# Issuing the K and V loads of a decode-attention kernel from GpSimd in place of SyncE

## The chip, the core and the metric

The kernel runs on one core of a Trainium2 chip. A core has five engines with instruction streams of their own, which meet only at semaphores: TensorE (PE: matmuls; PEld is its weight load), VectorE (DVE), ScalarE (ACT), GpSimd (POOL) and SyncE (SP), which issues transfers and computes nothing. The transfers between the device memory (DRAM) and the on-chip memory (SBUF, 128 partitions) are run by 16 DMA engines. Whoever issues a transfer puts it on a queue of its own: SP, ACT and POOL each have one. A transfer adds 16 to a semaphore when it has landed.

The metric is the device time of one execution in microseconds (us), the median of several runs.

## What is computed

One token is decoded by a gated mix of two parts: attention over a cache of 65536 keys and values for each of 32 heads, and a small feed-forward part.

```python
# x [1,1,512]; k_cache, v_cache [1,32,65536,128] bf16; wq [512,4096]; wo [4096,512]
q = (x @ wq).reshape(B, Sq, H, Dh).transpose(0, 2, 1, 3)
scores = jnp.einsum("bhqd,bhkd->bhqk", q, k_cache) * (Dh ** -0.5)
p = softmax(scores, axis=-1)
a = jnp.einsum("bhqk,bhkd->bhqd", p, v_cache).transpose(0, 2, 1, 3).reshape(B, Sq, H * Dh) @ wo
b = (silu(x @ w_gate) * (x @ w_up)) @ w_down          # 512 -> 1792 -> 512
g = sigmoid((x * gate_w).sum(-1, keepdims=True))
return g * a + (1 - g) * b
```

K and V together are 32 x 2 x 65536 x 128 x 2 bytes = 1074 MB, read once. Nearly everything that moves is K and V.

## The kernel before

**Tiles.** The keys of a head are cut into two halves of 32768 (A and B). A half of K or V is one load of 8 MB: each of the 128 partitions gets 256 rows of 128 numbers, 64 KB in one piece. The loads go to four regions of one SBUF buffer called `ring`: K_A, K_B, V_A, V_B. The regions overlap (K_B begins in the middle of K_A, V_B 16 KB into V_A), so a load has to wait until the part of its neighbour that it overwrites has been used.

**Work of one head.** DVE transposes K chunk by chunk, 16 chunks of 16 rows for each half (line 309, into four buffers `kt`), and counts them in the semaphore `ktd`, 32 to a head. PE turns each chunk into scores (line 396, into `psS`). After both halves DVE takes the maximum along each partition (line 333), POOL takes it across the partitions (line 213), ACT makes the exponentials with their sums (lines 246 and 248), POOL adds the sums across partitions (line 215), and DVE transposes the exponentials into `pb` (line 335). Then PE multiplies them with V: half A at once (line 412 in `flow`; the semaphore `va1` says that the rows from 64 on have been used), half B after the scores of the first K half of the next head (lines 412, 447 and 403; the semaphore `vbd` says that V_B has been used).

**PE's order.** PE goes through blocks: `pe_ka` (scores of half A), `pe_vb` (values of half B of the head before), `pe_kb` (scores of half B, then values of half A). Between the `pe_vb` of head 30 and the `pe_kb` of head 31 it goes through `pe_wo`: it waits for both halves of the matrix wo, does 32 matmuls with the outputs of heads 0 to 30 (line 423 in `whole`), and raises `s_wod`. After the `pe_kb` of head 31 comes `pe_mlp`, the feed-forward part, and then a last `pe_vb`.

```python
            with nc.body("pe_wo", valid_engines=only):
                pe.wait_ge(sm["s_otn"], H + 1)
                ...
                pe.wait_ge(sm["s_wo"], 32)
                for j in range(32):
                    last = whole(om[:, j:j + 1], wo_ap[:, j, :], first=(j == 0))
                last.then_inc(sm["s_wod"], 1)
                nc.br("pe_kb", engines=only)
```

**SP's order.** SP issues every large load, one after the other, each behind a wait: wq first, then K of head 0 in four half loads, V_A of head 0, and then for each head r (`head` in the listing) the K_A of head r + 1 (when half of K_B has been transposed), the V_B of head r (after `va1`), the K_B of head r + 1 (when half of K_A has been transposed), the V_A of head r + 1 (after `vbd`). For the last round the two halves of wo stand ahead of the K_B of head 31, each behind a wait for transposes that free its place. Then follow, as their places come free, the weights w_gate and w_up (after `s_wod`), the last rows of wo, w_down, and the V_B of head 31 in six pieces (`PARTS`): the first, 64 rows per partition, at once, and the other five after `va1` of head 31. Since all of them are on one queue, they move in this order.

**POOL's order.** It clears some buffers, copies four tiles into `sel` (line 208), and then does the two reductions of each head, each behind its wait. The other changes of place, and the lines that issue and wait, are in the listing.

Of the kernel before, what the change touches and what calls it, by code (L numbers as in the profile page):

```python
# [6 lines left out]
KB = 1024  # L7
CH = 16
NB = 4
K_A, K_B = 0, 32 * KB  # L10
V_A, V_B = 96 * KB, 112 * KB
# [6 lines left out]
ET = mybir.EngineType  # L18
# [8 lines left out]
def bass_gated_mix__mha_block_cached__swiglu_ffn__decode_kernel(  # L27
# [11 lines left out]
    out: bass.AP,  # L39
):  # L40
    _, H, S, Dh = A_k_cache.shape
    D = A_wq.shape[0]
    F = B_w_gate.shape[1]
    Dc = D // P
    FC = F // P
    ROWS = S // (2 * P)
    NCH = ROWS // CH
    SCALE = float(Dh) ** -0.5
    assert Dh == 128 and D == 512 and F % P == 0 and ROWS == 256 and H == 32
    L = H - 1  # L50
    A_ORDER = list(range(NCH // 2, NCH)) + list(range(NCH // 2))
    B_ORDER = list(range(NCH))
    PER = 2 * NCH

    with ExitStack() as ctx:
# [6 lines left out]
        def sem(name):  # L62
            return ctx.enter_context(nc.semaphore(name))
# [46 lines left out]
        sm = {n: sem(n) for n in names.split()}  # L110
# [4 lines left out]
        kv_dram = {"k": A_k_cache[0].rearrange("h (u p r) d -> h u p (r d)", u=2, p=P),  # L115
                   "v": A_v_cache[0].rearrange("h (u p r) d -> h u p (r d)", u=2, p=P)}

        def at(byte, n):
            return ring[:, byte // 2:byte // 2 + n]

        WQ, WO, WG, WU, WO1, WD = 144 * KB, 0, 0, 14 * KB, 28 * KB, 64 * KB
        PARTS = ((192, 256), (0, 64), (64, 128), (128, 168), (168, 184), (184, 192))
        FLOW = 3
        MARKS = ("s_vb", "s_p2", "s_p3", "s_p4", "s_p5", "s_p6")
# [16 lines left out]
        @block.sync  # L141
        def _(sp):
            def load(dst, src, s):
                sp.dma_start(dst, src).then_inc(sm[s], 16)  # L144

            def place(kind, h, u, s):
                byte = {"k": (K_A, K_B), "v": (V_A, V_B)}[kind][u]
                src = kv_dram[kind][:, u]
                if isinstance(h, int):
                    src = src[h]  # L150
                else:
                    src = src[bass.ds(h, 1)].rearrange("h p n -> (h p) n")
                load(at(byte, ROWS * Dh), src, s)

            k0 = kv_dram["k"][0, 0]
            k1 = kv_dram["k"][0, 1]
            half = ROWS * Dh // 2
            load(at(K_A + 2 * half, half), k0[:, half:2 * half], "s_ka")
            load(at(K_A, half), k0[:, 0:half], "s_k0a")
            load(at(K_B + 2 * half, half), k1[:, half:2 * half], "s_k0b")  # L160
            sp.wait_ge(sm["ktd"], NCH // 2)
            load(at(K_B, half), k1[:, 0:half], "s_kb")
            sp.wait_ge(sm["s_q"], 1)
            place("v", 0, 0, "s_va")

            def head(r, late):
                sp.wait_ge(sm["ktd"], r * PER + (PER - NCH // 2))
                place("k", r + 1, 0, "s_ka")
                sp.wait_ge(sm["va1"], r + 1)
                place("v", r, 1, "s_vb")  # L170
                if late:
                    wo_dram = A_wo.rearrange("(p j) n -> p (j n)", j=32)
                    for q in range(2):
                        sp.wait_ge(sm["ktd"], r * PER + (PER + 3 * NCH // 4 + q * NCH // 4))
                        load(at(WO + q * 16 * KB, 16 * D), wo_dram[:, q * 16 * D:(q + 1) * 16 * D], "s_wo")
                sp.wait_ge(sm["ktd"], r * PER + (PER + NCH // 2))
                place("k", r + 1, 1, "s_kb")
                sp.wait_ge(sm["vbd"], r + 2)
                place("v", r + 1, 0, "s_va")

            with nc.Fori(0, L - 1, engines=[ET.SP]) as i:
                head(i, False)
            head(L - 1, True)
            sp.wait_ge(sm["s_wod"], 1)
            load(at(WG, Dc * F), B_w_gate.rearrange("(p c) f -> p (c f)", c=Dc), "s_wg")
            load(at(WU, Dc * F), B_w_up.rearrange("(p c) f -> p (c f)", c=Dc), "s_wu")
            load(at(WO1, D), A_wo[L * Dh:H * Dh, :], "s_wo1")
            sp.wait_ge(sm["ktd"], PER * H)
            wd_dram = B_w_down.rearrange("(p c) n -> p (c n)", c=FC)
            load(at(WD, WD_CUT * D), wd_dram[:, 0:WD_CUT * D], "s_wd")  # L190
            last = kv_dram["v"][L, 1]
            for n, ((r0, r1), s) in enumerate(zip(PARTS, MARKS)):
                if n == 1:
                    sp.wait_ge(sm["va1"], H)
                load(at(V_B + r0 * 256, (r1 - r0) * Dh), last[:, r0 * Dh:r1 * Dh], s)
            for j, s in ((FC - 3, "s_wd1"), (FC - 2, "s_wd2"), (FC - 1, "s_wd3")):
                load(at(WD + 2 * j * D, D), wd_dram[:, j * D:(j + 1) * D], s)

        @block.gpsimd
        def _(pool):  # L200
            nc.gpsimd.memset(xTz[:], 0.0).then_inc(sm["s_qd"], 1)
            nc.gpsimd.memset(qd[:], 0.0).then_inc(sm["s_qd"], 1)
            for m, n in enumerate(MARKS[1:]):
                nc.gpsimd.memset(hbuf[:, m], 0.0).then_inc(sm[n], 16 * L)
            pool.wait_ge(sm["s_id"], 1)
            for je in range(4):
                off = 64 * (je // 2) + je % 2
                last = nc.gpsimd.tensor_copy(sel[:, je, :].rearrange("p (g d) -> p g d", g=4),
                                             ident[:, off:off + 63:2].unsqueeze(1).to_broadcast([P, 4, 32]))
            last.then_inc(sm["s_sel"], 1)  # L210
            for h in range(H):
                pool.wait_ge(sm["s_mx"], h + 1)
                nc.gpsimd.partition_all_reduce(amx, mxs, P, RMAX).then_inc(sm["s_ar"], 1)  # L213
                pool.wait_ge(sm["s_exp"], h + 2)
                nc.gpsimd.partition_all_reduce(Lt, rsum, P, RADD).then_inc(sm["s_L"], 1)  # L215

        @block.scalar
        def _(act):
# [330 lines left out]
```

## Time and profile before

| | us |
|---|---|
| median of 3 runs | 2518.72 (2518.53 to 2519.13) |
| the profiled execution, first to last instruction (its own time) | 2517.1 |
| DVE busy | 1249.7 (50%) |
| PE busy | 1500.6 (60%) |
| POOL busy | 25.5 (1%) |
| moved by the DMA queues | 1087.86 MB, mean 432 GB/s |

All times within the profile are microseconds from the start of this one execution. Rows of the timeline give the start, the duration, the engine, the line of the kernel, the operation with what it writes and reads, how many instructions were merged, and in brackets how long the engine had been idle before and what ended that. "SPq" and "ACTq" are issues of transfers: their duration is that of the issue, not that of the transfer, and a merged row spans the waits between its issues. A "q" with a number is a DMA queue: q1 is SP's, q10 ACT's.

### The profile page before, as it was taken

What the parts mean: (1) busy time and instruction counts of PE and PEld (TensorE: products, weight loads), DVE (VectorE), ACT (ScalarE), POOL (GpSimd) and SP (SyncE); (2) the same over time, 40 slices, a digit from 0 to 9 for tenths busy, and PEclk for the clock granted to TensorE, in tenths of its full rate; (3) what the DMA queues carried; (4) which work ended last, traced back from release to release, by engine and by line L of the source; (5) the groups of instructions that cost most, each with busy time, mean ns of one, the idle gap of its engine ahead of it and who ended that gap; (6) DMA issues with size and microseconds to landing.
All of it is one profiled execution on the core that took longest, in us unless ns stands there. A gap on an engine that the chain in (4) does not pass through costs nothing.

```text
span 2517.1 us, 25084 instructions
## 1 busy us (share of the span) xinstructions
PE 1500.6 (60%) x10126; PEld 572.7 (23%) x10126; DVE 1249.7 (50%) x1213; ACT 42.4 (2%) x141; POOL 25.5 (1%) x79
## 2 busy tenths in 40 slices
PE   4664654755656556556565575565655655656566
PEld 1221221212222222222222221222221222222222
DVE  5454553644545536445455354464553544545534
ACT  0000000000000000000000000000000000000000
POOL 0000000000000000000000000000000000000000
PEclk9877877877778777777787787777877778778778
DMA  9999999999999999999999999999999999999999
GB/s 419 435 434 436 433 434 433 434 434 434 433 433 433 434 433 433 433 433 433 432 433 433 433 433 433 433 433 433 433 433 433 433 433 433 434 433 433 433 432 395
DMA packets 20892, 1087.86 MB, mean 432 GB/s; under 512 B 2323, under 2 KB 2838, under 8 KB 3094
## 3 DMA queue, kind: packets, MB, share of 16 engines
q1 hardware_dynamic: 20880, 1087.78, 99.9%
q8 instruction: 4, 0.07, 0.0%
q14 instruction: 2, 0.02, 0.0%
q10 hardware_dynamic: 6, 0.00, 0.0%
HBM read 1087.77 MB, written 0.00 MB: 432 GB/s over the span
## 4 chain that ended last, share of the span: by engine, by line
DMA 75%; DVE 15%; issue 7%; PE 2%; DVEq 1%; SPq 0%; ACT 0%; POOL 0%
DMA ring<-in_A_k_cache_dram 74%; DVE kt L309 15%; PE psS L396 2%; DMA ring<-in_A_v_cache_dram 1%; DVEq L306 0%; SPq L144 0%; PE psW L412 0%; DVE st L320 0%; PE psY L418 0%; PE psO L403 0%; ACT pa L248 0%; DVE pb L335 0%; DVE st L333 0%; DVEq L319 0%; DVE fin L354 0%
## 5 line engine op out<-in xcount | busy, mean ns | idle before, releaser
L396 PE MATMUL psS<-kt,zq 128*128 128x512 bf16 x4096 | 1134.0, 426 | 865.1 <-DVE kt L309 847.0
L309 DVE STREAM_TRANSPOSE kt<-ring 128x1024 uint32<-128x1024 uint32 x1024 | 1163.2, 1206 | 939.9 <-DMA ring<-in_A_k_cache_dram 939.9
L396 PEld LDWEIGHTS psS<-kt,zq 128*128 128x128 bf16 x4096 | 387.2, 104 | 1598.5 <-DVE kt L309 1134.7
L412 PE MATMUL psW<-ring,pb 128*4 128x512 bf16 x3584 | 255.2, 447 | 104.0 <-DVE pb L335 102.3
L412 PEld LDWEIGHTS psW<-ring,pb 128*4 128x4 bf16 x3584 | 94.2, 98 | 263.4 <-issue 186.7
L322 DVE COPY brow<-psW 128x512 f32<-128x512 f32 x32 | 22.1, 690 | 120.4 <-PE psW L412 120.4
L403 PEld LDWEIGHTS psO<-pb,ring 128*128 128x128 bf16 x2048 | 57.0, 98 | 0.6 <-DMA ring<-in_A_v_cache_dram 0.5
L403 PE MATMUL psO<-pb,ring 128*128 128x1 bf16 x2048 | 56.6, 163 | 0.4 <-DMA ring<-in_A_v_cache_dram 0.2
L325 DVE TENSOR_SCALAR lt<-psO,st,sc 128x4 f32 x32 | 9.4, 294 | 89.2 <-PE psO L403 89.2
L447 PE MATMUL psO<-id,brow 128*128 128x1 f32 x256 | 33.7, 253 | 25.5 <-DVE brow L322 24.7
L335 DVE STREAM_TRANSPOSE pb<-pa 128x512 bf16<-128x512 bf16 x32 | 22.8, 711 | 48.7 <-ACT pa L248 48.7
L246 ACT ACTIVATE st<-st 128x1 f32<-128x1 f32 x32 | 6.5, 203 | 2383.2 <-POOL st L213 2383.2
L333 DVE TENSOR_REDUCE st<-psS 128x1 f32<-128x512 f32 x32 | 22.1, 692 | 37.5 <-PE psS L396 37.5
L447 PEld LDWEIGHTS psO<-id,brow 128*128 128x128 f32 x256 | 31.0, 191 | 41.7 <-DVE brow L322 40.4
L213 POOL PARTITION_ALL_REDUCE st<-st x32 | 11.2, 350 | 2420.6 <-DVE st L333 2420.6
L248 ACT ACTIVATE pa<-psS,st 128x512 bf16<-128x512 f32 x32 | 22.0, 687 | 1.0
L215 POOL PARTITION_ALL_REDUCE st<-st x32 | 12.3, 383 | 36.4 <-ACT pa L248 36.4
L423 PE MATMUL psF<-ring,om 128*1 128x512 bf16 x32 | 9.6, 474 | 2.8 <-DMA ring<-in_A_wo_dram 2.8
L253 ACT COPY zq<-qd 128x16 bf16 x31 | 7.7, 248 | 0.0
L248 ACT ACTIVATION_READ_ACCUMULATOR pa<-psS,st 128x1 f32 x32 | 6.2, 193 | 0.0
L423 PE MATMUL psF<-ring,kt 128*1 128x512 bf16 x11 | 3.9, 527 | 3.0 <-DVE kt L348 3.0
L350 DVE COPY brow<-psW 128x512 f32<-128x512 f32 x1 | 0.7, 690 | 9.8 <-PE psW L412 9.8
(82 smaller groups left out, 48.9 us busy)
## 6 DMA issues: line engine op xcount, KB each, us to landing
ring<-in_A_k_cache_dram SPq DMA_DIRECT2D x4, 4096.0 KB, 27.6
ring<-in_A_v_cache_dram SPq DMA_DIRECT2D x3, 2048.0 KB, 17.9
ring<-in_A_wq_dram SPq DMA_DIRECT2D x1, 4096.0 KB, 12.1
ring<-in_A_wo_dram SPq DMA_DIRECT2D x2, 2048.0 KB, 10.6
ring<-in_B_w_gate_dram SPq DMA_DIRECT2D x1, 1792.0 KB, 33.2
ring<-in_B_w_up_dram SPq DMA_DIRECT2D x1, 1792.0 KB, 37.2
ring<-in_B_w_down_dram SPq DMA_DIRECT2D x1, 1408.0 KB, 13.4
ring<-in_A_v_cache_dram SPq DMA_DIRECT2D x1, 1280.0 KB, 21.5
```

The source lines that it names most:

```text
L213: nc.gpsimd.partition_all_reduce(amx, mxs, P, RMAX).then_inc(sm["s_ar"], 1)
L215: nc.gpsimd.partition_all_reduce(Lt, rsum, P, RADD).then_inc(sm["s_L"], 1)
L248: nc.scalar.activation(pa[:], psS[:], ACT.Exp, bias=nbias, scale=SCALE, accum_out=rsum).then_inc(sm["s_exp"], 1)
L309: nc.vector.transpose(o, src).then_inc(sm["ktd"], 1)
L322: nc.vector.tensor_copy(brow[:], psW[:]).then_inc(sm["s_flc"], 1)
L333: nc.vector.reduce_max(mxs, psS[:], AX_X).then_inc(sm["s_mx"], 1)
L335: nc.vector.transpose(pb[:], pa[:]).then_inc(sm["s_pb"], 1)
L396: last = nc.tensor.matmul(psS[:], zw[je][c], ktb[n % NB][:, je // 2, :, je % 2], start=first and je == 0, stop=stop and je == 3)
L403: last = nc.tensor.matmul(psO[:, 0:1], at(base + r * 256, Dh), pb[:, col:col + 1], start=first and n == 0, stop=stop and n == len(rows) - 1)
L412: last = nc.tensor.matmul(psW[g:g + 4, :], pb[:, col:col + 97:32], at(base + r * 256, 4 * Dh), start=first and n < 4, stop=stop and n >= l ...
L423: return nc.tensor.matmul(psF[0:1, :], lhs, rhs, start=first, stop=stop)
L447: nc.tensor.matmul(psO[:, 0:1], brow[:, e * Dh:(e + 1) * Dh], id4[:, e:e + 1], start=e == 0, stop=False)
```

## The change

All K loads and all V loads but the last five pieces are issued by POOL, which also writes their descriptors (the lists of what is to be moved). POOL's program is written out for all heads: after the clearing and the copies into `sel` come the four half loads of K of head 0 and its V_A, and then for each round the four loads, with the same waits as on SP, and the two reductions of the head between the first of them and the second. The first piece of the last V follows on POOL without a wait, ahead of the reductions of head 31. SP keeps wq, both halves of wo (each behind its wait for transposes, but no longer in the row of the K loads), the weights of the feed-forward part, and the last five pieces of V after `va1` of head 31.

```diff
         @block.sync
...
-            def head(r, late):
-                sp.wait_ge(sm["ktd"], r * PER + (PER - NCH // 2))
-                place("k", r + 1, 0, "s_ka")
-                sp.wait_ge(sm["va1"], r + 1)
-                place("v", r, 1, "s_vb")
-                if late:
-                    wo_dram = A_wo.rearrange("(p j) n -> p (j n)", j=32)
-                    for q in range(2):
-                        sp.wait_ge(sm["ktd"], r * PER + (PER + 3 * NCH // 4 + q * NCH // 4))
-                        load(at(WO + q * 16 * KB, 16 * D), wo_dram[:, q * 16 * D:(q + 1) * 16 * D], "s_wo")
-                sp.wait_ge(sm["ktd"], r * PER + (PER + NCH // 2))
-                place("k", r + 1, 1, "s_kb")
-                sp.wait_ge(sm["vbd"], r + 2)
-                place("v", r + 1, 0, "s_va")
-
-            with nc.Fori(0, L - 1, engines=[ET.SP]) as i:
-                head(i, False)
-            head(L - 1, True)
+            wo_dram = A_wo.rearrange("(p j) n -> p (j n)", j=32)
+            for q in range(2):
+                sp.wait_ge(sm["ktd"], L * PER + (3 * NCH // 4 + q * NCH // 4))
+                load(at(WO + q * 16 * KB, 16 * D), wo_dram[:, q * 16 * D:(q + 1) * 16 * D], "s_wo")
             sp.wait_ge(sm["s_wod"], 1)
...
             load(at(WD, WD_CUT * D), wd_dram[:, 0:WD_CUT * D], "s_wd")
+            sp.wait_ge(sm["va1"], H)
             last = kv_dram["v"][L, 1]
-            for n, ((r0, r1), s) in enumerate(zip(PARTS, MARKS)):
-                if n == 1:
-                    sp.wait_ge(sm["va1"], H)
+            for (r0, r1), s in list(zip(PARTS, MARKS))[1:]:
                 load(at(V_B + r0 * 256, (r1 - r0) * Dh), last[:, r0 * Dh:r1 * Dh], s)
...
         @block.gpsimd
...
-            for h in range(H):
-                pool.wait_ge(sm["s_mx"], h + 1)
+
+            def fetch(kind, h, u, s):
+                byte = {"k": (K_A, K_B), "v": (V_A, V_B)}[kind][u]
+                nc.gpsimd.dma_start(at(byte, ROWS * Dh), kv_dram[kind][h, u]).then_inc(sm[s], 16)
+
+            def across(r):
+                pool.wait_ge(sm["s_mx"], r + 1)
                 nc.gpsimd.partition_all_reduce(amx, mxs, P, RMAX).then_inc(sm["s_ar"], 1)
-                pool.wait_ge(sm["s_exp"], h + 2)
+                pool.wait_ge(sm["s_exp"], r + 2)
                 nc.gpsimd.partition_all_reduce(Lt, rsum, P, RADD).then_inc(sm["s_L"], 1)
+
+            half = ROWS * Dh // 2
+            for u, byte, part, s in ((0, K_A, 1, "s_ka"), (0, K_A, 0, "s_k0a"), (1, K_B, 1, "s_k0b"), (1, K_B, 0, "s_kb")):
+                if s == "s_kb":
+                    pool.wait_ge(sm["ktd"], NCH // 2)
+                nc.gpsimd.dma_start(at(byte + 2 * part * half, half),
+                                    kv_dram["k"][0, u][:, part * half:(part + 1) * half]).then_inc(sm[s], 16)
+            pool.wait_ge(sm["s_q"], 1)
+            fetch("v", 0, 0, "s_va")
+            for r in range(L):
+                pool.wait_ge(sm["ktd"], r * PER + (PER - NCH // 2))
+                fetch("k", r + 1, 0, "s_ka")
+                across(r)
+                pool.wait_ge(sm["va1"], r + 1)
+                fetch("v", r, 1, "s_vb")
+                pool.wait_ge(sm["ktd"], r * PER + (PER + NCH // 2))
+                fetch("k", r + 1, 1, "s_kb")
+                pool.wait_ge(sm["vbd"], r + 2)
+                fetch("v", r + 1, 0, "s_va")
+            r0, r1 = PARTS[0]
+            nc.gpsimd.dma_start(at(V_B + r0 * 256, (r1 - r0) * Dh),
+                                kv_dram["v"][L, 1][:, r0 * Dh:r1 * Dh]).then_inc(sm["s_vb"], 16)
+            across(L)
```

More of the change, by code (lines that the diff above doesn't have):

```diff
@@ L144, in load @@
                 sp.dma_start(dst, src).then_inc(sm[s], 16)
[L146 to L164, printed above, removed]
-            def head(r, late):
-                sp.wait_ge(sm["ktd"], r * PER + (PER - NCH // 2))
-                place("k", r + 1, 0, "s_ka")
-                sp.wait_ge(sm["va1"], r + 1)
-                place("v", r, 1, "s_vb")
-                if late:
-                    wo_dram = A_wo.rearrange("(p j) n -> p (j n)", j=32)
-                    for q in range(2):
-                        sp.wait_ge(sm["ktd"], r * PER + (PER + 3 * NCH // 4 + q * NCH // 4))
-                        load(at(WO + q * 16 * KB, 16 * D), wo_dram[:, q * 16 * D:(q + 1) * 16 * D], "s_wo")
-                sp.wait_ge(sm["ktd"], r * PER + (PER + NCH // 2))
-                place("k", r + 1, 1, "s_kb")
-                sp.wait_ge(sm["vbd"], r + 2)
-                place("v", r + 1, 0, "s_va")
-            with nc.Fori(0, L - 1, engines=[ET.SP]) as i:
-                head(i, False)
-            head(L - 1, True)
+            wo_dram = A_wo.rearrange("(p j) n -> p (j n)", j=32)
+            for q in range(2):
+                sp.wait_ge(sm["ktd"], L * PER + (3 * NCH // 4 + q * NCH // 4))
+                load(at(WO + q * 16 * KB, 16 * D), wo_dram[:, q * 16 * D:(q + 1) * 16 * D], "s_wo")
             sp.wait_ge(sm["s_wod"], 1)
```

## The prediction

> **What bounds the kernel now.** I read the page first: the slices of DMA, the queues, the chain of waits. Then the DMA issues by line, and the timeline at three places: one head in the middle, the first 35 us, the last 100 us.
>
> ```profile
> span 2517.1 us, 25084 instructions
> ...
> DMA  9999999999999999999999999999999999999999
> GB/s 419 435 434 436 433 434 433 434 434 434 433 433 433 434 433 433 433 433 433 432 433 433 433 433 433 433 433 433 433 433 433 433 433 433 434 433 433 433 432 395
> ...
> q1 hardware_dynamic: 20880, 1087.78, 99.9%
> ...
> DMA 75%; DVE 15%; issue 7%; PE 2%; DVEq 1%; SPq 0%; ACT 0%; POOL 0%
> ```
>
> The transfers bound it from end to end: one queue, SP's, moves 1087.78 MB at 433 GB/s and holds 16 engines for 99.9% of the span; 1087.78 MB / 433 GB/s is 2512 of the 2517 us. So time can come back only from a higher rate, and each moment in which the engines have nothing queued is lost for good. A load of 8 MB (8.39 million bytes) takes 8.39 / 433 = 19.4 us. One partition's row of 64 KB, at 433 / 16 = 27.1 GB/s for one engine, takes 2.42 us, a row of 32 KB 1.21, one of 16 KB 0.61; a load gives each engine 8 rows. I take a row for a packet (125 whole loads of 128 rows are 16000 of the 20880 packets on q1).
>
> What keeps the queue full is how much of the load ahead is still to come when a load is issued. Two answers show it, the DMA issues (KB each, median us to landing) and the timeline of one head (start, duration):
>
> ```profile
> ring<-in_A_wq_dram SPq DMA_DIRECT2D x1, 4096.0 KB, 12.1
> ...
> ring<-in_A_v_cache_dram SPq DMA_DIRECT2D x63, 32.4
> ring<-in_A_k_cache_dram SPq DMA_DIRECT2D x62, 29.2
> ```
>
> ```profile
> 1164.95 0.33 SPq L144 DMA_DIRECT2D ring<-in_A_v_cache_dram  x1
> 1175.71 1.25 DVE L309 STREAM_TRANSPOSE kt<-ring 128x1024 uint32<-128x1024 uint32 x1 [16.48 <-DMA ring<-in_A_k_cache_dram]
> ...
> 1185.07 0.33 SPq L144 DMA_DIRECT2D ring<-in_A_k_cache_dram  x1
> 1194.98 2.77 PE L412 MATMUL psW<-ring,pb 128*4 128x512 bf16 x48
> ...
> 1201.23 0.33 SPq L144 DMA_DIRECT2D ring<-in_A_v_cache_dram  x1
> ...
> 1214.39 18.14 DVE L309 STREAM_TRANSPOSE kt<-ring 128x1024 uint32<-128x1024 uint32 x16 [12.76 <-DMA ring<-in_A_k_cache_dram]
> ...
> 1223.71 0.33 SPq L144 DMA_DIRECT2D ring<-in_A_k_cache_dram  x1
> ...
> 1234.49 0.35 POOL L213 PARTITION_ALL_REDUCE st<-st  x1 [75.53 <-DVE st L333]
> ...
> 1235.98 0.38 POOL L215 PARTITION_ALL_REDUCE st<-st  x1 [1.14 <-ACT pa L248]
> ```
>
> DVE or PE starts on a load the moment it has landed, so landings can be read from these rows: K at 1175.71, V at 1194.98, K at 1214.39, one load time (19.3) apart. The K issued at 1185.07 has 1194.98 - 1185.07 = 9.9 us of V still ahead of it; the V at 1201.23 has 13.2, the V at 1164.95 has 10.8, and a K that lands 29.2 after its issue waits 29.2 - 19.4 = 9.8. **The cover of every steady issue is about 9.8 us.**
>
> **The steady part of the change.** 130 issues go from SP to POOL: 4 half loads, 125 whole ones, and 64 rows per partition of the last V. Each waits for the same semaphore as on SP. POOL's two reductions now stand between them: the one for the maximum (0.35 us) starts 10.8 us after the K fetch at 1223.71, and the one for the sum (0.38) is over before the next V fetch, which waits for va1, set by matmuls that need the softmax anyway. So no wait becomes longer, as long as a fetch leaves POOL free within 10.8 us; if it doesn't, the softmax is late, and with it va1 and the V fetch. What one fetch costs POOL no row shows. From below it is SP's 0.33 us, from above 9.8, where the cover ends and each further microsecond is paid some 125 times. I take 0.4, by the nearest POOL rows (0.35 and 0.38), and cost it at zero: the load ahead hides it. The rate I leave at 433 GB/s, for the same rows on the same engines. The bounds of that are wide: if every load had to start into an empty engine, it would pay what wq pays, 12.1 us for 4.19 MB that need 9.7, so 2.4 us each; a higher rate than now I can't exclude either, two slices of the page show 435 and 436. Both ends are among the rivals.
>
> **The start.** SP keeps wq first; the four half loads of K now stand on POOL behind its clearing and its copies into sel.
>
> ```profile
> 0.73 0.39 SPq L135 DMA_DIRECT2D ring<-in_A_wq_dram  x1
> ...
> 1.29 0.21 ACTq L229 DMA_DIRECT2D gwrow<-in_gate_w_dram  x1
> ...
> 3.26 1.00 POOL L208 COPY sel<-ident 128x128 bf16<-128x128 bf16 x4 [1.65 <-DVE ident L288]
> 7.79 0.68 DVE L294 CUSTOM_DVE_ANT_0 xg<-xrow,gwrow 1x512 f32<-1x512 bf16 x1 [4.38 <-DMA gwrow<-in_gate_w_dram]
> ...
> 13.02 1.90 PE L376 MATMUL psY<-ring,xTz 128*32 128x512 bf16 x16 [3.90 <-DMA ring<-in_A_wq_dram]
> ...
> 20.04 0.26 ACT L227 COPY zq<-qd 128x16 bf16<-128x16 bf16 x1
> ...
> 25.68 9.02 PE L396 MATMUL psS<-kt,zq 128*128 128x512 bf16 x32 [7.53 <-DVE kt L309]
> ...
> 33.96 0.43 SPq L144 DMA_DIRECT2D ring<-in_A_v_cache_dram  x1
> ```
>
> POOL is free at 4.3, so K's rows are there by about 6, while wq alone holds the engines until 13: nothing stands empty. From 6 on wq shares with K, row by row (both 32 KB), and its last 7 us become 14: it is used at 20 instead of 13.0, q is ready at 27 instead of 20.3, and the first scores start 1.6 us late (27.3 against 25.7). The fourth half and the first V are then issued at about 35.5 instead of 33.9; wq and the first three halves, 16.8 MB, keep the engines busy until 1.2 + 38.7 = 40. Cost zero, with 4.5 us to spare.
>
> **The end.** Here the queues matter. SP keeps wo, which PE needs between the values of head 30 and the second half of the scores of head 31 (block pe_wo): PE waits there for both halves of wo, does 32 matmuls, and only then goes to pe_kb.
>
> ```profile
> 2427.89 4.83 SPq L144 DMA_DIRECT2D ring<-in_A_wo_dram  x2
> 2432.77 0.43 SPq L144 DMA_DIRECT2D ring<-in_A_k_cache_dram  x1
> 2433.44 2.77 PE L412 MATMUL psW<-ring,pb 128*4 128x512 bf16 x48
> ...
> 2439.78 0.33 SPq L144 DMA_DIRECT2D ring<-in_A_v_cache_dram  x1
> ...
> 2443.32 9.61 PE L423 MATMUL psF<-ring,om 128*1 128x512 bf16 x32 [2.79 <-DMA ring<-in_A_wo_dram]
> 2452.96 0.33 SPq L144 DMA_DIRECT2D ring<-in_B_w_gate_dram  x1
> ...
> 2462.67 18.15 DVE L309 STREAM_TRANSPOSE kt<-ring 128x1024 uint32<-128x1024 uint32 x16 [22.48 <-DMA ring<-in_A_k_cache_dram]
> 2463.98 17.98 PE L396 MATMUL psS<-kt,zq 128*128 128x512 bf16 x64 [11.05 <-DVE kt L309]
> ...
> 2481.22 10.65 SPq L144 DMA_DIRECT2D ring<-in_A_v_cache_dram  x6
> ...
> 2508.98 1.04 PE L412 MATMUL psW<-ring,pb 128*4 128x512 bf16 x16 [1.67 <-DMA ring<-in_A_v_cache_dram]
> ...
> 2512.07 2.27 PE L403 MATMUL psO<-pb,ring 128*128 128x1 bf16 x64 [0.21 <-DMA ring<-in_A_v_cache_dram]
> ...
> 2515.99 0.23 ACTq L265 DMA_DIRECT2D out_dram<-fin  x1
> ```
>
> And two pieces of the chain that ended last, in order of time (start, duration): va1's matmuls, and the last of SP's pieces of V behind them.
>
> ```profile
> 2485.15 4.48 PE psW L412 x48
> ...
> 2490.96 22.35 DMA ring<-in_A_v_cache_dram
> ```
>
> Before, the order of the one queue put wo ahead of the last K: V landed at 2433.4, wo (2 x 2.1 MB, 9.7 us) at 2443.3, PE was done with it at 2452.9, and still waited until 2463.98 for K. There is a slack of 2463.98 - 2452.93 = 11 us. After, K is on POOL's queue, fetched some 9.4 us after the first transpose of its head and not behind wo; wo is on another queue, beside K and then beside the V fetched near 2440.
>
> How two queues share an engine only one row of before shows: gwrow, 1 KB on ACT's queue, issued at 1.29 into engines full of wq and used at 7.79, 6.5 us; the output, 1 KB from an idle queue, is there 1.1 us after its issue (2515.99 to the span's end). The difference, 5.4 us, is four to five rows of 32 KB, for a load with one data packet and one completion in an engine; far less than the queue ahead (38.7 us), and less than 8 rows (9.7). So I take turns, one row of each queue. wo's first row comes about 1.2 us after its issue (half of what wq shows above its transfer), at 2429.1. Each engine has 16 rows of wo, 16 KB each, and each goes with one of POOL's 64 KB: 16 x (2.42 + 0.61) = 48.5 us. POOL's queue has 2 rows of V, 8 of K and 8 of V for it, so there is always a partner. wo is complete at 2429.1 + 48.5 = **2477.6**, PE is done with it at 2477.6 + 9.61 = 2487.2, and the scores that started at 2463.98 start 23.2 us later. All behind them moves along: the softmax, va1 (which releases SP's last five pieces of V), the feed-forward part, the last values. Only the two waits for V at 2508.98 and 2512.07 (1.67 + 0.21 us) go: the five pieces go out from 2489.6 + 23.2 = 2512.8 on, need 1.2 us to start and 6.3 MB / 433 = 14.5 us, and are all there at about 2529; PE comes to the first for which it waited before at 2508.98 - 1.67 + 23.2 = 2530.5. wg and wu, behind the wait for wo on SP (2452.96, now 2487), take 8.5 us and are there before PE needs them. Sum: 2517.1 + 23.2 - 1.9 = 2538.4. The runs' median is 1.6 above the profiled span (2518.72 against 2517.1), so **2540**.
>
> [...]
>
> **The rivals.**
> *POOL's queue keeps an engine for a whole load.* wo's rows then come behind everything that POOL has queued: V until 2433.4, K 19.4, V 19.4, the 64 rows of the last V 4.8, wo itself 9.7: complete at 2486.7, 9.1 later than above, so 30.4 over before in place of 21.3. At the start wq's last rows come behind three halves of K, at 40; q is ready at 47, the fourth half is issued four transposes later at about 53, and the engines are empty for 13 us. 2518.7 + 30.4 + 13 = 2562. For it: nothing in the rows on POOL's queue; against it: gwrow.
> *wo is served in time.* If the queues share by bytes, wo takes 2 x 9.7 us from 2429.1 and is there at 2448.5, and PE is done at 2458.1, before K. The point that decides is 2463.98 - 9.61 = 2454.4. Then nothing moves: 2518.7, no change. For it: no row has two queues of long rows; against it: gwrow again, which waited longer than a fair share by bytes would let 1 KB wait.
> *POOL's queue is slower.* A rate lower by 1% costs 25 us: with the end 2565. At 2.4 us a load it is 125 x 2.4 = 300, so 2840. The same follows where a fetch takes over 9.8 us, for instance held up by the transposes beside it (the 8 left after a K fetch run for 8 x 18.14 / 16 = 9.1 us, just within the cover). For it: no row of a POOL load; against it: nothing of the rows' size or engines changes.
> *Faster.* Only by the rate: 436 throughout in place of 433 would give 17 us, and with wo in time 2502.
>
> **How the numbers follow.** Turns by single rows 0.50 (2540; with wo's first row up to two packets later or a packet earlier, 2532 to 2548); whole loads 0.13 (2562); wo in time 0.13 (2518.7); slower queue 0.18, half of it ending under 2575; faster 0.06. A change under 0.2% (5 us) can't be told from none here. Faster 0.06, same 0.13, slower 0.81. From 2517 to 2575 lie the first three and half of the fourth, 0.85.
>
> **What the profile after would show.** Right: slices of 433 GB/s and DMA at 9 until the last, then an empty stretch before SP's last V pieces; PE waiting in L423's group for wo some 35 us instead of 2.8; the second half of the scores of head 31 at 2487. K and V still landing 29 and 32 us after issue, POOL's fetches a few tenths. The forecast is wrong if the slices in the middle fall under 433, if wq is used after 30, or if wo is used before 2454.

## The result, and the profile after

The changed kernel takes 2539.4 us (median; 2539.0 to 2540.8) against 2518.8 before: a ratio of 1.0083 (95% interval 1.0071 to 1.0095), so 20.6 us slower. The forecast was 2540.

The page of the changed kernel shows where not to look:

```profile
span 2537.8 us, 24721 instructions
...
DMA  9999999999999999999999999999999999999996
GB/s 426 430 431 433 440 432 431 433 436 435 432 432 431 440 432 431 433 438 434 431 433 434 437 432 431 432 440 432 431 433 437 435 431 433 432 439 430 433 433 253
...
q0 software_dynamic: 18720, 1067.46, 97.2%
q1 hardware_dynamic: 2160, 20.32, 2.0%
...
L416 PE MATMUL psF<-ring,om 128*1 128x512 bf16 x32 | 9.9, 483 | 39.6 <-DMA ring<-in_A_wo_dram 39.6
```

97.2% of the engines' time now belongs to q0, POOL's queue. The slices read 426 to 440 GB/s until the last one, which falls to 253; the 38 between the first and the last have a mean of 433.5, against 433.3 before. In the last row PE sat idle 39.6 us until wo had landed, where it waited 2.8 before. The timeline of the same head as before shows that the steady part did not move by more than 0.1 us:

```profile
1164.97 0.57 POOL L179 DMA_DIRECT2D ring<-in_A_v_cache_dram  x1 [6.10 <-PE psW L405]
1175.62 1.25 DVE L302 STREAM_TRANSPOSE kt<-ring 128x1024 uint32<-128x1024 uint32 x1 [16.48 <-DMA ring<-in_A_k_cache_dram]
...
1185.11 0.53 POOL L179 DMA_DIRECT2D ring<-in_A_k_cache_dram  x1 [19.57 <-DVE kt L302]
1194.88 2.77 PE L405 MATMUL psW<-ring,pb 128*4 128x512 bf16 x48
...
1214.30 18.14 DVE L302 STREAM_TRANSPOSE kt<-ring 128x1024 uint32<-128x1024 uint32 x16 [12.76 <-DMA ring<-in_A_k_cache_dram]
```

The two halves of K here land at 1175.62 and 1214.30; before it was 1175.71 and 1214.39. The POOL fetches take 0.53 to 0.57 us, and 9.8 us of the load ahead (1194.88 - 1185.11) still cover the K fetch in these rows; the median of the 62 K loads is 29.1 us from issue to landing, so 9.7 above a transfer of 19.4. At 2414 the two kernels are still level, as this row of the kernel before shows:

```profile
2414.17 1.25 DVE L309 STREAM_TRANSPOSE kt<-ring 128x1024 uint32<-128x1024 uint32 x1 [16.48 <-DMA ring<-in_A_k_cache_dram]
```

What follows, in the changed kernel, is the whole difference:

```profile
2414.09 1.25 DVE L302 STREAM_TRANSPOSE kt<-ring 128x1024 uint32<-128x1024 uint32 x1 [16.48 <-DMA ring<-in_A_k_cache_dram]
...
2423.58 0.53 POOL L179 DMA_DIRECT2D ring<-in_A_k_cache_dram  x1 [20.59 <-DVE kt L302]
2427.81 4.83 SPq L144 DMA_DIRECT2D ring<-in_A_wo_dram  x2
2433.97 2.77 PE L405 MATMUL psW<-ring,pb 128*4 128x512 bf16 x48 [0.55 <-DMA ring<-in_A_v_cache_dram]
...
2458.29 4.62 DVE L302 STREAM_TRANSPOSE kt<-ring 128x1024 uint32<-128x1024 uint32 x4 [17.65 <-DMA ring<-in_A_k_cache_dram]
2480.55 9.87 PE L416 MATMUL psF<-ring,om 128*1 128x512 bf16 x32 [39.59 <-DMA ring<-in_A_wo_dram]
2490.35 15.89 PE L389 MATMUL psS<-kt,zq 128*128 128x512 bf16 x64
2490.45 0.33 SPq L144 DMA_DIRECT2D ring<-in_B_w_gate_dram  x1
...
2513.93 2.29 SPq L144 DMA_DIRECT2D ring<-in_A_v_cache_dram  x5
...
2536.72 0.23 ACTq L258 DMA_DIRECT2D out_dram<-fin  x1
```

The second half of K of the last head lands at 2458.3, 4.4 us earlier than before. DVE transposes four chunks, all that the buffers hold, and stops: PE stands in front of wo, issued at 2427.8 and used at 2480.55. The scores start at 2490.35 in place of 2463.98, and all that waits for them or for wo on SP goes out as much later. Meanwhile the engines run dry. The windows of the end show it. Each row has the length, the busy time of PE, PEld, DVE, ACT and POOL with the number of instructions, PE's granted clock, the share of the DMA engines and GB/s:

```profile
2440.00:2480.00 40.00, 0.46 (x12) 0.27 (x9) 4.92 (x5) 0.18 (x1) 1.04 (x2) 0.52 1.00 429
2480.00:2490.00 10.00, 9.45 (x31) 3.18 (x32) 0.00 (x0) 0.00 (x0) 0.00 (x0) 0.69 0.46 195
2490.00:2500.00 10.00, 10.00 (x45) 3.99 (x44) 8.53 (x8) 0.00 (x0) 0.00 (x0) 1.00 0.83 334
2500.00:2520.00 20.00, 16.56 (x115) 4.61 (x117) 8.04 (x11) 1.52 (x4) 0.73 (x2) 0.91 0.52 197
2520.00:2537.80 17.80, 11.83 (x151) 5.06 (x143) 5.29 (x7) 0.94 (x2) 0.00 (x0) 0.89 0.63 261
```

Until 2480 the DMA engines are full and PE does next to nothing; then PE works and the DMA engines are full for 0.46 to 0.83 of the time. Their unused time from 2480 on is 10 x 0.54 + 10 x 0.17 + 20 x 0.48 + 17.8 x 0.37 = 23.3 us. The kernel before keeps them at 0.97 and 1.03 in the two windows from 2480 to 2500, and leaves some 4 us unused in all, nearly all of it in its last window:

```profile
2500.00:2517.10 17.10, 11.69 (x143) 5.28 (x143) 1.51 (x4) 0.94 (x2) 0.00 (x0) 0.80 0.78 320
```

### The profile page after: what moved, and what is told of

Same layout as the page of the kernel before. It is cut to its first block, busy times and chain, and to the rows that moved or that the text cites. A ratio compares the mean times of both kernels' runs of the same rounds, so it can differ in the third digit from the quotient of the medians.

```text
span 2537.8 us, 24721 instructions
## 1 busy us (share of the span) xinstructions
PE 1498.7 (59%) x10126; PEld 572.5 (23%) x10126; DVE 1249.9 (49%) x1213; ACT 42.4 (2%) x141; POOL 95.5 (4%) x209
## 3 DMA queue, kind: packets, MB, share of 16 engines
q0 software_dynamic: 18720, 1067.46, 97.2%
## 4 chain that ended last, share of the span: by engine, by line
DMA 73%; DVE 15%; issue 7%; PE 3%; DVEq 0%; ACT 0%; POOL 0%
DMA ring<-in_A_k_cache_dram 72%; DVE kt L302 15%; PE psS L389 2%; DMA ring<-in_A_wo_dram 2%; PE psF L416 1%; DVEq L299 0%; PE psW L405 0%; DVE st L313 0%; PE psY L475 0%; DVE kt L336 0%; PE psO L396 0%; PE psY L411 0%; PE psO L440 0%; POOL sel L173 0%; ACT pa L241 0%
## 5 line engine op out<-in xcount | busy, mean ns | idle before, releaser
L179 POOL DMA_DIRECT2D ring<-in_A_k_cache_dram x62 | 32.7, 528 | 1317.2 <-DVE kt L302 1317.2
L179 POOL DMA_DIRECT2D ring<-in_A_v_cache_dram x63 | 34.5, 548 | 650.9 <-PE psO L396 473.9
L416 PE MATMUL psF<-ring,om 128*1 128x512 bf16 x32 | 9.9, 483 | 39.6 <-DMA ring<-in_A_wo_dram 39.6
## 6 DMA issues: line engine op xcount, KB each, us to landing
ring<-in_A_wo_dram SPq DMA_DIRECT2D x2, 2048.0 KB, 38.2
```

Of the source, the lines that this page charges most:

```text
L179: nc.gpsimd.dma_start(at(byte, ROWS * Dh), kv_dram[kind][h, u]).then_inc(sm[s], 16)
L416: return nc.tensor.matmul(psF[0:1, :], lhs, rhs, start=first, stop=stop)
```

## The experiments

The theory: the loss is wo, taking turns row by row with K and V because it is on another queue, and PE's work queued behind its wait for wo. The main rivals: POOL's own queue costs time; queues share in another way; or sharing makes the transfers slower.

**wo back in the row of K and V, on POOL.**

```diff
+                if r == L - 1:
+                    for q in range(2):
+                        pool.wait_ge(sm["ktd"], r * PER + (PER + 3 * NCH // 4 + q * NCH // 4))
+                        nc.gpsimd.dma_start(at(WO + q * 16 * KB, 16 * D), wo_dram[...]).then_inc(sm["s_wo"], 16)
                 pool.wait_ge(sm["ktd"], r * PER + (PER + NCH // 2))
                 fetch("k", r + 1, 1, "s_kb")
```

> The changed kernel, but POOL also issues both halves of wo, in the place they had in SP's order (after the V_B of head 30, before the K_B of head 31), so that wo shares a queue with K and V again. My theory (the whole loss is wo taking turns with the K and V rows on another queue): wo is used at about 2444 in place of 2480.6, PE is done with it before K lands, and the loss goes: 2519 to 2521 us (up to 1 us may stay, since w_gate and w_up still run beside the last V_A). Rival (POOL's queue or its descriptors cost time all along): the loss stays for the most part, 2530 to 2540.

Measured: 2519.0 us, a ratio to before of 1.0002 (0.9992 to 1.0011). The whole loss is gone while POOL issues every K and V load. From the timeline:

```profile
2428.18 0.53 POOL L201 DMA_DIRECT2D ring<-in_A_wo_dram  x1 [24.07 <-DVE kt L304]
...
2443.32 9.36 PE L418 MATMUL psF<-ring,om 128*1 128x512 bf16 x32 [2.89 <-DMA ring<-in_A_wo_dram]
...
2464.28 18.14 DVE L304 STREAM_TRANSPOSE kt<-ring 128x1024 uint32<-128x1024 uint32 x16 [24.17 <-DMA ring<-in_A_k_cache_dram]
...
2487.85 5.84 PE L407 MATMUL psW<-ring,pb 128*4 128x512 bf16 x64 [4.29 <-DMA ring<-in_A_v_cache_dram]
```

wo is used at 2443.32, the same instant as before. The last K and V land 1.6 and some 2.7 us later than PE took them up before (w_gate and w_up run beside them on SP's queue), and that costs nothing that can be measured.

**The reverse: no GpSimd at all, wo on ACT's queue.** The kernel before, with K and V on SP.

```diff
+            for q in range(2):
+                act.wait_ge(sm["ktd"], L * PER + (3 * NCH // 4 + q * NCH // 4))
+                act.dma_start(at(WO + q * 16 * KB, 16 * D), wo_dram[...]).then_inc(sm["s_wo"], 16)
             act.wait_ge(sm["s_o"], 1)
```

> The kernel before, with all K and V on SP, but with both halves of wo issued by ACT, behind the same waits, so on a queue beside SP's; POOL issues nothing. My theory: the loss needs no GpSimd at all, only wo on a second queue: wo used at about 2480, 2537 to 2541 us. Rival (POOL's queue is what takes the engines first): wo on ACT's queue gets a larger share, is used before 2454, and the time stays at 2519.

Measured: 2539.5 us (ratio 1.0085, 1.0068 to 1.0102), the time of the changed kernel to 0.1 us.

```profile
2480.86 9.74 PE L422 MATMUL psF<-ring,om 128*1 128x512 bf16 x32 [39.55 <-DMA ring<-in_A_wo_dram]
```

wo is used at 2480.86, 0.3 us from where the changed kernel has it. So the loss needs neither POOL nor its queue (q0, software_dynamic on the page; ACT's q10 and SP's q1 are hardware_dynamic), only wo on a second queue.

**The size of a row.** In the changed kernel wo's rows are 16 KB. With turns by rows, the length of a row would decide how much wo gets for each 64 KB of the other queue.

```diff
-            for q in range(2):
-                sp.wait_ge(sm["ktd"], L * PER + (3 * NCH // 4 + q * NCH // 4))
-                load(at(WO + q * 16 * KB, 16 * D), wo_dram[:, q * 16 * D:(q + 1) * 16 * D], "s_wo")
+            sp.wait_ge(sm["ktd"], L * PER + NCH)          # one load, rows of 32 KB
+            load(at(WO, 32 * D), wo_dram, "s_wo")
```

The other version has four loads of 8 KB rows, two behind each of the waits of the changed kernel.

> The changed kernel, with wo as one load with rows of 32 KB in place of two with rows of 16 KB, issued where the second half was (about 2432.4). If the engines take turns row by row, whatever the size of a row, 8 turns of 2.42 + 1.21 us from about 2436 on end at 2465, PE is done at 2475, the scores that started at 2490.4 start 15.4 us earlier: 2524 us. If the queues share by bytes, or wo just stands behind what POOL has queued, the size of a row doesn't matter: 2539.

> The changed kernel, with wo as four loads with rows of 8 KB. By turns, 32 rows are due: 18 go with POOL's rows of 64 KB (2.42 + 0.31 us each, to about 2480), 8 with its last 16 KB rows, 6 alone: wo complete at about 2489.5, 9 us later than in the changed kernel: 2548 us. By bytes, or behind POOL's queue: 2539 as it was.

Measured: 2524.2 us with 32 KB (ratio 1.0023, 1.0014 to 1.0033) and 2547.0 with 8 KB (1.0110, 1.0093 to 1.0127). The DMA issues of the two (count, KB each, median us to landing), and where PE takes wo up:

```profile
ring<-in_A_wo_dram SPq DMA_DIRECT2D x1, 4096.0 KB, 32.9
...
2432.59 0.33 SPq L144 DMA_DIRECT2D ring<-in_A_wo_dram  x1
...
2465.68 9.47 PE L415 MATMUL psF<-ring,om 128*1 128x512 bf16 x32 [25.04 <-DMA ring<-in_A_wo_dram]
```

```profile
ring<-in_A_wo_dram SPq DMA_DIRECT2D x4, 1024.0 KB, 49.5
...
2487.05 9.44 PE L417 MATMUL psF<-ring,om 128*1 128x512 bf16 x32 [46.31 <-DMA ring<-in_A_wo_dram]
```

The same 4.2 MB are used at 2465.7, 2480.6 and 2487.1 with rows of 32, 16 and 8 KB. The load with long rows is issued 4.8 us after the first half of the other, and lands 15 us earlier. Neither sharing by bytes nor a place behind POOL's queue gives that. 8 KB came 2.4 us earlier than worked out (2489.5).

The profiler's records of single rows show the turns themselves. From 2433 to 2479 the changed kernel moves 238 rows of wo and 245 rows of 64 KB, and the version with wo on ACT's queue 240 and 244. At the start of the changed kernel, where wq and K both have rows of 32 KB and all 16 engines are in step, 16 rows of K begin between 8.51 and 9.06, 16 of wq between 9.72 and 10.27, 16 of K between 10.93 and 11.48, and so on until wq is through.

**PE's work behind the wait.** The changed kernel, with PE's blocks in another order: after the small matmuls of pe_wo come the scores, then the wait and the matmuls with wo, then the values.

```diff
                 for n, c in enumerate(B_ORDER):
                     scores(NCH + n, NCH + c, i, False, n == NCH - 1)
+                nc.br_lt(left, 3, on_true="pe_wo", on_false="pe_kv", engines=only)
+
+            with nc.body("pe_kv", valid_engines=only):
```

> The changed kernel, with wo late on SP's queue as it is there, but PE does the second half of the scores of head 31 before it waits for wo, and the values of half A after it. My theory: the loss comes from the work queued behind PE's wait for wo, not from moving wo beside K and V as such. The scores run from about 2460 to 2478, the softmax under the wait, wo from 2480.6 to 2490.4, the values to 2496; va1 comes at about 2495 in place of 2514, but w_gate and w_up still wait for wo (2490.5), so the engines are empty for some 5 us: 2521 to 2526. If the transfers themselves had become slower by sharing, the loss stays near 2539.

Measured: 2526.1 us (ratio 1.0029, 1.0017 to 1.0040), at the upper end of what was expected.

```profile
2459.75 17.97 PE L389 MATMUL psS<-kt,zq 128*128 128x512 bf16 x64 [18.64 <-DVE kt L302]
...
2480.66 9.50 PE L416 MATMUL psF<-ring,om 128*1 128x512 bf16 x30 [2.94 <-DMA ring<-in_A_wo_dram]
...
2490.62 0.33 SPq L144 DMA_DIRECT2D ring<-in_B_w_gate_dram  x1
...
2502.45 3.41 PE L479 MATMUL psY<-ring,xTz 128*32 128x448 bf16 x16 [8.41 <-DMA ring<-in_B_w_up_dram]
```

wo is as late as in the changed kernel (2480.66), but PE's wait for it is 2.94 us, and 13.3 of the 20.6 us are back. What is left goes with the other thing behind wo: w_gate and w_up overwrite its place, so their issue stays at 2490.6, and the feed-forward part waits 8.4 us for them, where the kernel before waited 0.2. No run moved them by themselves.

**The cover.** The forecast costed the steady fetches at nothing, because the load ahead hides them. These runs take that cover away: the 62 steady K loads are issued later by a number of transposes of 1.13 us. The edit is shown for POOL; in the kernel before, SP's two waits change in the same way.

```diff
-                pool.wait_ge(sm["ktd"], r * PER + (PER - NCH // 2))
+                pool.wait_ge(sm["ktd"], r * PER + PER)                  # 8 transposes later
...
-                pool.wait_ge(sm["ktd"], r * PER + (PER + NCH // 2))
+                pool.wait_ge(sm["ktd"], r * PER + (PER + NCH))
```

> The kernel before, with the 62 steady K loads issued 8 transposes later (8 x 1.13 = 9.1 us), so that of the cover of 9.8 us about 0.7 is left. Whatever a fetch from SP needs from its issue to its first bytes beyond 0.7 us now shows 62 times. By the 2.4 us that wq shows at the start as the most: (2.4 - 0.7) x 62 = 105 us at most; if a fetch starts within 0.7 us, nothing. I expect 20 to 100 us: 2540 to 2620. If the cover were not what hides the fetch (an order of the queue that does not depend on it), nothing would change.

> The same delay of the K loads, in the version in which POOL issues K, V and wo. The difference to the late loads from SP, over 62, is what a fetch from POOL costs more until its first bytes. By the durations of the issues (0.53 us on POOL, 0.33 on SP) 0.2 us x 62 = 12 us more than from SP; if writing the descriptors has a hidden part, more: at 1 us each 62 more. If it is as quick as SP's, the two are equal.

> The version in which POOL issues K, V and wo, with the 62 steady K loads issued 4 transposes later (4 x 1.13 = 4.5 us) in place of 8. With 8 the late loads cost 129.7 us more than the version without delay, 2.1 us each, so a fetch from POOL needs 9.1 + 2.1 - 9.8 = 1.4 us beyond... in all about 2.8 us with the 0.7 of cover that was left. With 4 the cover left is 9.8 - 4.5 = 5.3 us, more than that: nothing is lost, 2518 to 2521. If every delay of a K load were paid in part (no threshold), half the loss: about 2583.

| K loads issued later by | from SP | from POOL (wo there too) |
|---|---|---|
| 0 | 2518.7 | 2519.0 |
| 4 transposes, 4.5 us | | 2519.4 |
| 8 transposes, 9.1 us | 2622.7 | 2648.7 |

4.5 us cost nothing (1.0002, 0.9993 to 1.0012), 9.1 us cost 104 us from SP and 130 from POOL, 1.68 and 2.09 us for each K load. From SP that is just above the range that was expected (2540 to 2620), and all but 1 of the 105 us that were named as the most. POOL's 26 us on top are more than twice the 12 that the durations of the issues gave. The DMA issues show the steady K loads: from POOL 4.5 us late, from POOL 9.1 us late, and from SP 9.1 us late.

```profile
ring<-in_A_k_cache_dram POOLq DMA_DIRECT2D x62, 24.6
```

```profile
ring<-in_A_k_cache_dram POOLq DMA_DIRECT2D x62, 22.2
```

```profile
ring<-in_A_k_cache_dram SPq DMA_DIRECT2D x62, 21.9
```

A K load that is 9.1 us late lands 21.9 us after its issue from SP and 22.2 from POOL, 2.5 and 2.8 more than its 19.4 of transfer. So in these runs the cover worked by a threshold: 9.8 us of it were there, 5.3 were still enough, 0.7 were not, and under 3 were needed, from either engine.

The records of single rows say what the loss consists of. In the late runs the engines stand empty for 0.96 us (SP) and 1.39 us (POOL) between the last rows of V and the first rows of K, and each engine's first row of K takes 3.1 us in place of 2.4 (medians over the K loads). The two together, 1.67 and 2.09 us, are what each K load was seen to cost. Counted from the start of the issue, the first row begins after 0.97 us from SP and 1.24 from POOL. That is 0.27 of the (130 - 104) / 62 = 0.42 us that a load from POOL cost more; for the rest, POOL's issue came 0.16 us later against the end of V's rows. A hidden part of the writing of descriptors, for which 1 us each had been allowed, stands in no row by itself: of POOL's work for a fetch the rows show the issue of 0.53 to 0.57 us, on a queue listed as software_dynamic.

## Why the prediction was right

- **The end carries all of it: right.** The kernels are level to 0.1 us at 2414, and putting wo back on the queue of K and V brings the loss to nothing.
- **Turns row by row: right, and shown by the size of a row and by the records of single rows.** wo was forecast to be complete at 2477.6 and was used at 2480.55. The step that was short is the first turn, taken at 1.2 us after the issue from what wq shows: the records have the first row of wo at 2431.15, 3.3 us after its issue, just where a row of POOL's that had begun at 2428.73 ends. The turns themselves, from there to the end of the last row at 2479.78, take 48.6 us, against 48.5 in the forecast.
- **PE waits, and the scores move by 23.2 us: right in kind, 26.4 measured.** That the sum still came out (20.7 in the span against 21.3) is partly luck. The scores took 15.89 us in place of 17.98, because four chunks lay transposed and waiting, which the forecast had overlooked, and the work behind them took 31.6 us in place of 35.1. Of these 3.6 us, 1.9 are the two waits for V that were forecast to go. The forecast left the other waits for transfers in: the kernel before also waits for w_up, for V once more, and twice for w_down, 0.22 + 0.22 + 0.30 + 0.18 = 0.9 us in the rows below, and the changed kernel has none of these waits. No row accounts for the last 0.8 us. PE's granted clock was higher too, 0.89 in the last window against 0.80 before; whether that has a part in it was not tested.

```profile
2490.68 3.43 PE L482 MATMUL psY<-ring,xTz 128*32 128x448 bf16 x16 [0.22 <-DMA ring<-in_B_w_up_dram]
...
2513.36 0.90 PEld L403 LDWEIGHTS psO<-pb,ring 128*128 128x128 bf16 x24 [0.22 <-DMA ring<-in_A_v_cache_dram]
...
2514.70 0.08 PEld L418 LDWEIGHTS psY<-ring,kt 128*1 128x1 bf16 x1 [0.30 <-DMA ring<-in_B_w_down_dram]
...
2514.97 0.08 PEld L418 LDWEIGHTS psY<-ring,kt 128*1 128x1 bf16 x1 [0.18 <-DMA ring<-in_B_w_down_dram]
```

- **The steady part costs nothing: right.** A fetch was taken at 0.4 us and takes 0.53 to 0.57; the late loads show that the cover, not a small price, is the reason. Of the 38 slices between the first and the last, 18 read 430 to 432 GB/s, and slices under 433 had been named as a sign that the forecast is wrong. That sign was drawn too tight: the others read up to 440, the mean is that of before, and the landings stay where they were.
- **The start costs nothing: right, with wq early.** wq was forecast at 20 and used at 17.97, because K's first rows came at 8.5 us and not at 6 and so left it the engines alone for longer. The first scores are at 25.36, 0.3 us before those of the kernel before, not 1.6 after.

```profile
17.97 1.90 PE L369 MATMUL psY<-ring,xTz 128*32 128x512 bf16 x16 [8.93 <-DMA ring<-in_A_wq_dram]
...
25.36 8.92 PE L389 MATMUL psS<-kt,zq 128*128 128x512 bf16 x32 [2.30 <-DVE kt L302]
```

- **The rivals.** A whole load at a time (2562) fell: POOL's queue gave way row by row, 238 rows of wo against 245 of 64 KB from 2433 to 2479. wo in time fell with the landing at 2480. The slower queue and the faster one both fell with 2519.0 for the version with K, V and wo on POOL.

## What to carry to other kernels

Before moving loads to another queue, look at what the order of the one queue did for the loads that stay: here a small load that had a place in the row became one that got a turn per row, and its time was the number of its rows on each engine times the sum of one of its rows and one of the other queue (16 x (2.42 + 0.61) = 48.5 us, 48.6 measured). Give such a load long rows (2524.2 us here in place of 2539.4), keep it on the queue of the bulk (2519.0), or put nothing behind its wait (2526.1 with the scores ahead of it). Who issued the bulk loads hardly mattered here (2519.0 from POOL with wo there too, 2518.7 from SP) as long as each issue came well before the load ahead was through (under 3 us were needed here); measure that cover first.

## What the runs showed of the hardware that was not expected

Three row sizes of the same matrix beside rows of 64 KB gave 32.9 us to landing for 32 KB, 38.2 for the halves with 16 KB and 49.5 for the quarters with 8 KB (medians over the loads of a version; the middle one is the changed kernel's), and POOL's queue (q0, software_dynamic) took the same turns as SP's (q1, hardware_dynamic): wo was used at 2480.55 beside POOL's queue and at 2480.86 beside SP's.

```profile
ring<-in_A_wo_dram SPq DMA_DIRECT2D x2, 2048.0 KB, 38.2
```

PE's granted clock did not simply follow its rest: it was 0.52 in the 40 us of near idleness, 0.69 in the 10 us after them and 1.00 in the next 10. The kernel before, without such a rest, was granted 0.98 in the same window from 2490 to 2500. What sets it stays open.
